# New landing margins, a later start for the transposes of x, and a fourth buffer pair in the last window, in the plan of an attention-plus-SSM kernel

## The chip, the core and the metric

One core of a Trainium2 chip runs the whole kernel. The core has five engines with an instruction queue each: TensorE (PE in the profile; PEld is its loading of weights), VectorE (DVE), ScalarE (ACT), GpSimd (POOL) and SyncE (SP). SP here only issues transfers between HBM and on-chip memory. TensorE's results land in PSUM banks, and the other engines read them there. An engine takes its instructions strictly in the order in which the program lists them; between engines there are semaphores. The metric is the time of one execution in device microseconds, lower is better, as the median of several runs. A profiled execution gives the trace from which all other numbers come.

## The reference

Two branches read the same x of 2048 x 512: softmax attention with 32 heads of 16 columns, and a state space layer (S4), that is, a convolution of every column with a kernel of 2048 steps that is built from 128 complex modes. A gate mixes the two.

```python
def _A_ref(x, wqkv, wo):
    ...
    scale = Dh ** -0.5
    scores = jnp.einsum("bhqd,bhkd->bhqk", q, k) * scale
    p = _softmax(scores, axis=-1)
    o = jnp.einsum("bhqk,bhkd->bhqd", p, v)
    return (lambda x, *d: x.transpose(*d))(o, 0, 2, 1, 3).reshape(B, S, D) @ wo

def _B_ref(u, A_re, A_im, B_re, B_im, C_re, C_im, log_dt, Dskip):
    ...
    P = jnp.exp(logdA[:, :, None] * l[None, None, :])
    K = jnp.einsum("dn,dnl,dn->dl", Cc, P, dB).real
    ...
    Yf = Uf * Kf[None, :, :, :]
    y = ...irfft2(Yf)[:, :, 0, :L]
    y = (lambda x, *d: x.transpose(*d))(y, 0, 2, 1) + u * Dskip[None, None, :]
    return y

x = A_x
g = _sigmoid((x * gate_w).sum(-1, keepdims=True))
a = _A_ref(x, A_wqkv, A_wo)
b = _B_ref(x, B_A_re, B_A_im, B_B_re, B_B_im, B_C_re, B_C_im, B_log_dt, B_Dskip)
return g * a + (1 - g) * b
```

## The kernel before

**Attention.** The scores of 32 heads, 2048 queries and 2048 keys are cut into 2048 tiles of 128 keys x 512 queries, in 32 blocks of 64 tiles; a block is four heads over 512 queries. The loop at the end of `record()` walks over 683 score groups. For each group g, `qk(g)` puts three tiles of scores into one of two PSUM buffers, SC (PE, matmul SC<-Qm,KT), and `ex(g)` lets ACT take the exponential of them into a slot of ET (line 907, ET<-SC). `pv()` then multiplies the tiles with the values, into the PSUM bank OA (PE, OA<-ET,VE). At a block's end DVE transposes OA into OT (line 978), which frees OA for the next block, and normalises: a reciprocal Rz (984), a product ON (990), and, for each pair of blocks, a second transpose into OnT (997). The masked queries Qm of a block, four rows each, are loaded by SP from gm_qd (line 735), where SP stored them before from Qs (line 1597).

**Tiles that DVE takes.** Part of the exponentials is not ACT's. A *set* is four tiles of one key tile; in each of four groups one of the three tiles belongs to the set, so that ACT's exponential there is narrow (128x1024 instead of 128x1536) and DVE turns the third tile into the bits of an exponential by one operation of 0.66 us on the scores (line 943, DZ<-SC; a *bit row* below). After the fourth bit row two *steps* (line 954, DU<-DZ and DZ<-DZ, 128x2048) refine it, each followed by matmuls into OA. A set's DZ and DU are one of the buffer pairs of its window. `WIN` lists the windows: first group, group after the last, number of buffer pairs, and how many lists of key tiles may be used. Before, there are 63 sets in three windows, 30, 5 and 28 of them. `dvq()` gives the idle time that DVE must have gathered in the plan before another set starts, by the phase the program is in (`DVQ`), and `keytile()` takes the next key tile from the current block's list while more than `LEFT` of them remain, and from the next block's otherwise.

**The state space branch** runs in the gaps of PE and on DVE. `params()` and `base()` make tables of powers. `table()` then builds 16 blocks of the powers in PT, two at a time: two copies that begin a pair (line 1222), complex products (line 1001), and one store for each block, gm_ptd<-PT (line 1239, SP). As there is one PT for a pair, the two copies of the next pair overwrite what the stores read, and wait for them. `kstage()` multiplies PT with the modes' weights (bank MB), evicts Kst (lines 1272 and 1273) and stores it in gm_kpd (line 1277). `qload()` reads the stored table back transposed (Qt, line 1251), `sstage()` makes the states SG (line 1304), `scan()` carries them along time (lines 1328 to 1342). Last come 32 *y units*: `yload()` brings Py from gm_ptd (line 1360) and four Tt from gm_kpd (line 1366), three units ahead at most; PE forms y in MB (MB<-Py,SG, then MB<-Tt,XY), DVE evicts it to Yst (line 1415), and SP stores it in gm_ytd (line 1420). XY, x in another order, is loaded by `xload()` (line 1441). `turned()` makes a transposed x: eight rounds of two transposing reads XR<-gm_xrd (line 1455) and four stores gm_xcd<-XR (line 1459), through two buffers; `ublocks()` reads it (X2, line 1469). At the end y comes back transposed (`yread()`, Yl, line 1433), the gated attention of three quarters comes back as AR (`reload()`), and `outs()` adds the two (line 1565, AR<-AR,Yl). The fourth quarter goes through the last copies behind the last exponential.

**What sets the order.** Nothing of this order is written out by hand. While the program is recorded, `Prog` keeps a planned clock for every engine and a planned end for every operation, and `Sched` holds the side work as threads of segments, each with an engine, a cost and a priority. After every exponential, `fill()` issues side work until the planned clock of ACT. It takes the segment that could start first; a segment's start is `est()`, the later of its engine's clock and `ready()`, the planned end of all that it needs. For a transfer `ready()` adds a margin to the planned landing: the one given with the transfer (`m=`), otherwise `DMARG`. So the margins delay no instruction by themselves. They decide what stands ahead of it in its engine's queue. On the chip an instruction then waits for the real landing. The two places where the margins stand:

```python
t = max(t, self.fin[(s, i)] + (.03 if s == eng else self.marg.get((s, i), DMARG) if isinstance(s, tuple) else DLAG if eng == 'PE' and s == 'DVE' else .05))
...
[(PT, i, blk)], [(ptd, blk)], c=.84, lat=4.1, m=PTM)
```

Of the kernel before, what the change touches and what calls it, by code (L numbers as in the profile page):

```python
# [24 lines left out]
ZCOL = .216 / 512  # L25
FILL = 3500
EVERY = 2
XAT = "pt0"
HWIN = 3.0
OVER = .6  # L30
DLAG = 0.6
TURN = dict(F=.105, R=.105, C=.105, H=.06)
DMARG = 1.2
PTM = 2.4
ZLAG = .6
BARE = 1
NS = 15
# [5 lines left out]
XB = 128 * (127 - math.log2(3.15037))  # L43
VKT = ((1, 5, 9, 13), (3, 7, 11))
SHAPE = ((2, 1),) * 4
LEFT = 3
VSW = 152
VSP = [len(k) * VSW for k in VKT]
VSAT = (158, 500)
WIN = ((170, 475, 2, 1), (475, 540, 3, 1), (540, 678, 3, 2))  # L50
DVQ = (("scan1", 0.2), ("scan0", 0.5), ("S15", 1.0), (None, 0.5))
BP = 2.2
DVCAP = 2.0
BUP = 1
# [33 lines left out]
class Prog:  # L88
# [65 lines left out]
    def ready(self, a):  # L154
        eng, R, W = a[1][0], a[1][2], a[1][3]
        t = 0.0
        for acc, wr in ((R, False), (W, True)):
            for b, sl, *tag in acc:
# [5 lines left out]
                for d in (st[0], st[1]) if wr else (st[0],):  # L164
                    for s, i in d.items():
                        if s != "PE" or eng != "PE":
                            t = max(t, self.fin[(s, i)] + (.03 if s == eng else self.marg.get((s, i), DMARG) if isinstance(s, tuple) else DLAG if eng == 'PE' and s == 'DVE' else .05))
        return t
# [52 lines left out]

    def dma(self, eng, fn, R=(), W=(), c=.45, lat=3.0, m=DMARG):
        if self.cap is not None:
            self.cap.append((self.dma, (eng, fn, R, W), dict(c=c, lat=lat, m=m)))
            return
        self.log.append((self.dma, self.q, (eng, fn, R, W)))
        k = self.dnext
        self.dnext = (k + 1) % NDSEM
        s = ("D", k)
        deps = self._deps(s, R, W)  # L230
        if self.dn[k]:
            deps[s] = max(deps.get(s, -1), self.dn[k])
        at = self.tm[eng]
        for s2, k2 in deps.items():
            at = max(at, self.fin[(s2, k2)] + .08)
        self.tm[eng] = at + c
        self.dn[k] += 1
        self.fin[(s, self.dn[k])] = at + c + lat
        self.marg[(s, self.dn[k])] = m
        self._record(eng, fn, deps, s, self.dn[k], R, W)  # L240
# [172 lines left out]
def declare(nc, es):  # L413
    B = {}

    def sb(name, free, dt=BF16):
        B[name] = Buf(name, "sb", free, dt)
# [9 lines left out]
    sb("ET", NS * 512)  # L427
    for w, (_, _, n, _) in enumerate(WIN):
        for r in range(n):
# [180 lines left out]
def record(nc, p, B, ins):  # L610
# [135 lines left out]
    def dvq():  # L746
        return next(n for f, n in DVQ if f is None or f in sch.flag)

    def win(x):
        return next((w for w, (lo, hi, _, _) in enumerate(WIN) if lo <= x < hi), None)  # L750

    def keys(x):
        w = win(x)
        return () if w is None else sum(VKT[:WIN[w][3]], ())

    def clear(x):
# [3 lines left out]
        mine = [i for i, st in enumerate(sets) if st["w"] == w]  # L760
        return len(mine) < WIN[w][2] or f"dvp{mine[-WIN[w][2]]}" in sch.flag

# [4 lines left out]
    def keytile(x):  # L767
        of = rem if len(rem) > LEFT else ahead
        return next(((of, q) for q in of if q % 16 in keys(x)), None)
# [27 lines left out]
    def decide(g):  # L797
        while len(tiles) < min(3 * g + 3, NSL):
            x = len(tiles) // 3
            plan["used"] = max(plan["used"], idle() - DVCAP)  # L800
            if plan["set"] is None and clear(x) and idle() - plan["used"] >= dvq():
# [3 lines left out]
                w = win(x)  # L805
                r = f"{w}{sum(st['w'] == w for st in sets) % WIN[w][2]}"
                old = [i for i, st in enumerate(sets) if st["r"] == r]
# [398 lines left out]
    def table():  # L1206
# [3 lines left out]
        for pb in range(NBLK // 2):  # L1210
# [26 lines left out]
            for i, blk in enumerate(blks):  # L1237
                yield ("SP", .5, 2)
                dma("SP", lambda e, i=i, blk=blk: e.dma_start(ptd.dram(blk * P * PTN, [[PTN, P], [1, PTN]]), PT(i * PTN, [[1, PTN]])),
                    [(PT, i, blk)], [(ptd, blk)], c=.84, lat=4.1, m=PTM)  # L1240
                sch.mark(f"pt{blk}")
# [203 lines left out]
    def turned():  # L1445
        XR, xcd = B["XR"], B["xcd"]
        for z in range(4):
            yield ("SP", .6)
            dma("SP", lambda e, z=z: e.dma_start(xcd.dram(z // 2 * P * 8192 + z % 2 * 4096 + 64 * (1 - z % 2), [[8192, P], [P, 32], [1, 64]]), wm(0, [[0, 32], [1, 64]])),
                [(wm, 0)], [(xcd, ("z", z))], c=.6, lat=6.)  # L1450
        yield ("AFTER", XAT)
        for c in range(8):
# [359 lines left out]
```

## Time and profile before

| | us |
|---|---|
| three timed runs | 850.25, 851.02, 852.69 (median 851.02) |
| the profiled execution | 850.08 |
| its span, first to last instruction | 848.3 |
| mean granted clock of TensorE | 0.982 of full speed |

The span by stages, in busy us of each engine (the view that cuts the span into windows):

| stage | span | PE | DVE | ACT | share of DMA time |
|---|---|---|---|---|---|
| start, projections, 0 to 60 | 60 | 46.5 | 45.6 | 54.3 | 0.79 |
| 60 to 200 | 140 | 109.0 | 134.6 | 140.0 | 0.36 |
| table and states, 200 to 475 | 275 | 227.2 | 260.0 | 267.9 | 0.63 |
| scans and y units, 475 to 680 | 205 | 170.8 | 193.1 | 197.8 | 0.48 |
| last y units, end, 680 to 848 | 168 | 148.9 | 149.5 | 161.2 | 0.36 |

How to read the lines below: the page gives each engine's busy time, share of the span and number of instructions. The chain of waits follows the work that ended last back from its end, at each step to what released it. A timeline row has the start and the duration in us, engine, source line, operation, output<-input, shapes, how many it stands for, and in brackets how long the engine was idle ahead of it and what ended that. A row of the groups has busy us and mean ns of one after the bar, then the idle time ahead of them with what ended most of it.

### The profile page before, as it was taken

Reading aid. Unit: us, or ns where it says so; the run is one execution under the profiler, and the core shown is the slowest. Engines: PE = TensorE matmul, PEld = TensorE weight load, DVE = VectorE, ACT = ScalarE, POOL = GpSimd, SP = SyncE. Lnnn points to the kernel's source line nnn. Section 1 sums busy time; section 2 is a strip of 40 time slices with the busy share of each in tenths; the row PEclk is TensorE's granted clock in tenths of the full one; section 3 lists DMA queues with packets and bytes.
Section 4 is the critical chain, followed back from the end, with each engine's and each line's share of the span. In section 5 each row is a group of like instructions: output and inputs, shape, how many; then the busy total and the mean of one; then the engine's idle time right before and its main releaser. Section 6 shows DMA issues by size and latency. Waiting matters only on the chain.

```text
span 848.3 us, 20990 instructions
## 1 busy us (share of the span) xinstructions
PE 702.4 (83%) x8959; PEld 255.5 (30%) x8984; DVE 782.8 (92%) x1338; ACT 821.2 (97%) x695; POOL 11.0 (1%) x13
## 2 busy tenths in 40 slices
PE   7787777777768989887788887798977779999986
PEld 3232332222112333332232332344422224434322
DVE  5799999998888999999999999999879999899995
ACT  7999999999889999999999999999979999999996
POOL 4000000000000000000000000000000000000000
PEclk9999999999899999999999999999879999999999
DMA  9750003965572568895491880166763014645203
GB/s 199 155 73 11 10 3 136 167 200 137 127 196 101 100 110 199 134 203 115 131 138 33 162 150 5 34 137 166 160 151 94 5 54 114 136 103 130 60 15 121
DMA packets 247953, 94.90 MB, mean 112 GB/s; under 512 B 222644, under 2 KB 234804, under 8 KB 245812
## 3 DMA queue, kind: packets, MB, share of 16 engines
q1 hardware_dynamic: 245988, 92.51, 49.5%
q10 hardware_dynamic: 1872, 1.05, 0.6%
q8 instruction: 70, 1.15, 0.5%
q14 instruction: 23, 0.19, 0.1%
HBM read 33.08 MB, written 35.01 MB: 80 GB/s over the span
## 4 chain that ended last, share of the span: by engine, by line
ACT 75%; DVE 11%; PE 5%; DMA 5%; SPq 2%; issue 1%; ACTq 0%; DVEq 0%
ACT ET L907 75%; DVE DZ L943 2%; PE OA L626 2%; PE SC L626 2%; DMA gm_ptd<-PT 2%; DVE tt L1001 1%; PE MB L626 1%; DMA Wk<-in_A_wqkv_dram 1%; DMA XR<-gm_xrd 1%; DVE PT L1001 1%; DMA Py<-gm_ptd 1%; DVE SG L1304 1%; SPq L1459 1%; DVE s L1331 1%; DVE ft L1001 1%
## 5 line engine op out<-in xcount | busy, mean ns | idle before, releaser
L907 ACT ACTIVATE ET<-SC 128x1536 bf16<-128x1536 f32 (+1 forms) x683 | 812.7, 1522 | 14.1 <-PE SC L626 13.6
L626 PE MATMUL SC<-Qm,KT 32*128 32x512 bf16 x2048 | 283.0, 389 | 114.8 <-ACT ET L907 99.6
L626 PE MATMUL OA<-wm 128*32 128x512 bf16 (+3 forms) x1376 | 205.8, 368 | 1.2 <-DVE wm L679 1.2
L626 PE MATMUL OA<-ET,VE 128*32 128x512 bf16 x1796 | 181.9, 397 | 6.5 <-DVE OT L978 5.9
L943 DVE TENSOR_SCALAR DZ<-SC 128x512 uint16<-128x512 f32 x252 | 167.1, 683 | 11.3 <-PE SC L626 10.6
L626 PEld LDWEIGHTS SC<-Qm,KT 32*128 32x128 bf16 x2048 | 72.4, 91 | 331.8 <-ACT ET L907 285.2
L626 PEld LDWEIGHTS OA<-ET,VE 128*32 128x32 bf16 x1796 | 46.0, 93 | 108.8 <-issue 98.3
L626 PEld LDWEIGHTS OA<-wm 128*32 128x32 bf16 (+2 forms) x1376 | 54.8, 96 | 25.5 <-issue 16.7
L954 DVE TENSOR_SCALAR DZ<-DZ 128x2048 uint16<-128x2048 uint16 x63 | 43.2, 686 | 6.5 <-PE OA L626 6.4
L1304 DVE TENSOR_SCALAR SG<-MB 128x512 bf16<-128x512 f32 x64 | 43.9, 685 | 2.7 <-PE MB L626 2.3
L626 PE MATMUL MB<-X,Qt 128*128 128x64 bf16 x512 | 42.7, 244 | 0.0
L954 DVE TENSOR_SCALAR DU<-DZ 128x2048 uint16<-128x2048 uint16 x63 | 42.6, 684 | 0.1
L1339 DVE TENSOR_TENSOR G<-s,s 128x512 f32<-128x512 f32 x60 | 41.2, 687 | 1.0
L1331 DVE TENSOR_TENSOR s<-G,MU 128x512 f32<-128x512 f32 x60 | 41.1, 684 | 0.0
L1336 DVE TENSOR_TENSOR s<-s,SG 128x512 f32<-128x512 f32 x60 | 41.0, 684 | 0.0
L1333 DVE TENSOR_TENSOR s<-G,MU 128x512 f32<-128x512 f32 x60 | 41.0, 683 | 0.0
L626 PEld LDWEIGHTS MB<-X,Qt 128*128 128x128 bf16 x512 | 28.8, 116 | 19.6 <-issue 19.6
L1001 DVE TENSOR_TENSOR ft<-FP,L 128x1024 f32<-128x1024 f32 (+1 forms) x32 | 34.2, 1086 | 0.1
L1001 DVE TENSOR_TENSOR PT<-tt,tt 128x1024 bf16<-128x1024 bf16 x48 | 32.8, 682 | 0.2
L626 PE MATMUL MB<-Py,SG 128*32 128x64 bf16 x1024 | 29.1, 234 | 3.3 <-DMA Py<-gm_ptd 3.3
L626 PEld LDWEIGHTS MB<-Py,SG 128*32 128x32 bf16 x1024 | 27.8, 168 | 11.1 <-issue 5.2
L978 DVE STREAM_TRANSPOSE OT<-OA 128x512 f32<-128x512 f32 x32 | 22.7, 709 | 4.1 <-PE OA L626 3.8
(167 smaller groups left out, 614.7 us busy)
## 6 DMA issues: line engine op xcount, KB each, us to landing
gm_ptd<-PT SPq DMA_DIRECT2D x16, 1024.0 KB, 5.7
Py<-gm_ptd SPq DMA_DIRECT2D x32, 512.0 KB, 4.5
gm_kpd<-Kst SPq DMA_DIRECT2D x16, 256.0 KB, 3.8
Tt<-gm_kpd SPq DMA_DIRECT2D x128, 32.0 KB, 3.3
gm_xrd<-in_A_x_dram SPq DMA_DIRECT2D x1, 2048.0 KB, 12.2
gm_xcd<-wm SPq DMA_DIRECT2D x4, 512.0 KB, 11.9
gm_xcd<-XR SPq DMA_DIRECT2D x32, 64.0 KB, 2.4
Wo<-in_A_wo_dram SPq DMA_DIRECT2D x4, 512.0 KB, 4.4
```

Of the source, the lines that this page charges most:

```text
L626: op("PE", lambda t: t.matmul(out(), lhsT(), rhs(), start=start, stop=stop, skip_group_check=True, **kw), R, W, c=c, lat=.15, a=a, cfg=cfg)
L907: op("ACT", lambda a: a.activation(ET(512 * e, [[1, 512 * n]]), sc(0, [[1, 512 * n]]), AF.Exp, scale=DH ** -0.5), [(sc, i, g) for i in ran ...
L943: op("DVE", lambda v: v.tensor_scalar(z.u16(512 * k, [[1, 512 * n]]), sc(512 * na, [[1, 512 * n]]), XS, XB, ALU.mult, ALU.add), [(sc, na + ...
L954: op("DVE", lambda v: v.tensor_scalar(t.u16(0, [[1, 2048]]), z.u16(0, [[1, 2048]]), float(STEP[k][0]), None, ALU.add), R, W, c=.07 + 2048 ...
L978: op("DVE", lambda v: v.transpose(OT(512 * w, [[1, 512]]), OA(0, [[1, 512]])), [(OA, 0, b)], [(OT, w, b)], c=.64)
L1001: op(eng, lambda v: v.tensor_tensor(o(), a(), b_(), f), R, W, c=c)
L1304: op("DVE", lambda v, kh=kh, part=part: v.tensor_scalar(sg(2 * SGH + SGH * part + CB * k8 + 16 * kh, [[2 * SGH, 32], [1, 16]]), MB(0, [[16 ...
L1331: op(e, lambda v: v.tensor_tensor(s2(0, W), G(0, W), MU(d0, [[0, 2], [1, 256]]), ALU.mult), key("G", "MU"), [(s2, 0)], c=F5)
L1333: op(e, lambda v: v.tensor_tensor(s3(0, W), G(256, [[-256, 2], [1, 256]]), MU(D + d0, [[D, 2], [1, 256]]), ALU.mult), key("G", "MU") + [(M ...
L1336: op(e, lambda v, so=so: v.tensor_tensor(s2(0, W), s2(0, W), sg(so, [[SGH, 2], [1, 256]]), ALU.add), [(s2, 0)] + ks, [(s2, 0)], c=F5)
L1339: op(e, lambda v: v.tensor_tensor(G(0, [[1, 512]]), s2(0, [[1, 512]]), s3(0, [[1, 512]]), ALU.add), [(s2, 0), (s3, 0)], [(G, 0)], c=F5)
L1459: dma("SP", lambda e, c=c, cc=cc: e.dma_start(xcd.dram(cc % 2 * P * 8192 + cc // 2 * (4096 + 64) + 4 * c * P, [[8192, P], [P, 4], [1, 64]] ...
```

## The change

Six numbers of the plan change; the operations and their planned costs stay.

```diff
-XAT = "pt0"
+XAT = "base0"
...
-DMARG = 1.2
-PTM = 2.4
+DMARG = 2.4
+PTM = 5.0
...
-LEFT = 3
+LEFT = 4
...
-WIN = ((170, 475, 2, 1), (475, 540, 3, 1), (540, 678, 3, 2))
-DVQ = (("scan1", 0.2), ("scan0", 0.5), ("S15", 1.0), (None, 0.5))
+WIN = ((170, 475, 2, 1), (475, 540, 3, 1), (540, 678, 4, 2))
+DVQ = (("scan1", 0.0), ("scan0", 0.5), ("S15", 1.0), (None, 0.5))
```

`DMARG` and `PTM` are the margins above: `PTM` that of the table's store, `DMARG` that of every other transfer. `XAT` is the event after which `turned()` may begin; base0 comes ahead of the first table pair. `LEFT` and `DVQ` belong to the choice of sets: a set's key tile comes from the next block while four or fewer key tiles of the current one remain, and behind the second scan DVE need not have gathered any idle time. The last window gets a fourth pair of DZ and DU. Since every choice of `fill()` depends on those before it, the order of all engines changes from the first table pair on. Now 64 sets are formed, 28, 6 and 30 in the three windows; ACT has 426 wide and 257 narrow exponentials, where it had 430 and 253.

Three places, as the order of the program lists them (line, operation, output<-inputs, shape, and x for how many in a row; numbers behind a name tell buffers of one kind apart).

DVE ahead of the refill of PT behind the table's fourth stores, before (PT's last product is the first row of line 1001 shown, FP and L make the next table, B holds what the copies read):

```order
L1001 TENSOR_TENSOR PT<-tt_167,tt_168 128x2x32x16
L929 TENSOR_SCALAR VS_54<-VE 128x608 x3
L1001 TENSOR_TENSOR ft_161<-FP,L_140 128x1024
L1272 CAST Kst<-MB 128x8x64
L1273 TENSOR_SCALAR Kst<-MB,Dp 128x8
L1001 TENSOR_TENSOR B_165<-ft_160,ft_161 128x64x8 x2
L1272 CAST Kst<-MB 128x8x64
L1273 TENSOR_SCALAR Kst<-MB,Dp 128x8
L1198 CAST B_165<-FP 128x256x8
L1222 COPY PT<-B_164 128x64x16 x2
```

The same engine and place now; the rows end with the copy, and the last product into PT stands above them:

```order
L1272 CAST Kst<-MB 128x8x64
L1273 TENSOR_SCALAR Kst<-MB,Dp 128x8
L984 RECIPROCAL Rz<-OT 128x32
L990 TENSOR_TENSOR ON<-OT,Rz 128x2x16x16
L943 TENSOR_SCALAR DZ_57<-SC 128x512
L997 STREAM_TRANSPOSE OnT_75<-ON 128x512
L943 TENSOR_SCALAR DZ_57<-SC 128x512
L943 TENSOR_SCALAR DZ_59<-SC 128x512 x4
L954 TENSOR_SCALAR DU_58<-DZ_57 128x2048
L954 TENSOR_SCALAR DU_60<-DZ_59 128x2048
L1222 COPY PT<-B_166 128x64x16
```

Eight bit rows and two steps of two sets, two Kst evictions and a normalisation now stand between the store and the copy that waits for it, in place of the products for the next table and two Kst evictions.

SP around the loads of the y unit that ran at 617 us, before:

```order
L1360 DMA Py_184<-gm_ptd 128x2x1024
L1366 DMA Tt_185<-gm_kpd 64x4x64 x2
L1420 DMA gm_ytd<-Yst_186 128x4x64
L1366 DMA Tt_185<-gm_kpd 64x4x64 x2
L1441 DMA XY2_181<-gm_xrd 64x32x64 x2
L1420 DMA gm_ytd<-Yst_186 128x4x64
L1360 DMA Py_184<-gm_ptd 128x2x1024
L1366 DMA Tt_185<-gm_kpd 64x4x64
L735 DMA Qm_52<-gm_qd 16x512 x4
L630 DMA Wo2_85<-in_A_wo_dram 128x4x512
L1420 DMA gm_ytd<-Yst_186 128x4x64
L1366 DMA Tt_185<-gm_kpd 64x4x64 x3
```

SP at the same place now:

```order
L1360 DMA Py_186<-gm_ptd 128x2x1024
L735 DMA Qm_52<-gm_qd 16x512 x4
L630 DMA Wo2_87<-in_A_wo_dram 128x4x512
L1420 DMA gm_ytd<-Yst_188 128x4x64
L1366 DMA Tt_187<-gm_kpd 64x4x64 x4
L1420 DMA gm_ytd<-Yst_188 128x4x64
L1360 DMA Py_186<-gm_ptd 128x2x1024
L1366 DMA Tt_187<-gm_kpd 64x4x64 x4
L1420 DMA gm_ytd<-Yst_188 128x4x64
L1360 DMA Py_186<-gm_ptd 128x2x1024
L1366 DMA Tt_187<-gm_kpd 64x4x64 x4
L1441 DMA XY2_183<-gm_xrd 64x32x64
```

The four Qm, Wo2 and the loads of XY2 no longer stand between a unit's Py and its last Tt: the first two stand a unit earlier, XY2 two units later.

DVE in the last stretch, before:

```order
L943 TENSOR_SCALAR DZ_67<-SC 128x512 x3
L1565 TENSOR_TENSOR AR_78<-AR_78,Yl 128x2048
L1565 TENSOR_TENSOR AR_81<-AR_81,Yl 128x2048
L1565 TENSOR_TENSOR AR_84<-AR_84,Yl 128x2048
L954 TENSOR_SCALAR DU_70<-DZ_69 128x2048
L954 TENSOR_SCALAR DU_72<-DZ_71 128x2048
L954 TENSOR_SCALAR DU_68<-DZ_67 128x2048
L954 TENSOR_SCALAR DZ_69<-DZ_69 128x2048
L954 TENSOR_SCALAR DZ_71<-DZ_71 128x2048
```

DVE in the same stretch now:

```order
L943 TENSOR_SCALAR DZ_73<-SC 128x512 x2
L943 TENSOR_SCALAR DZ_67<-SC 128x512 x3
L1565 TENSOR_TENSOR AR_83<-AR_83,Yl 128x2048
L943 TENSOR_SCALAR DZ_67<-SC 128x512
L1565 TENSOR_TENSOR AR_86<-AR_86,Yl 128x2048
L954 TENSOR_SCALAR DZ_69<-DZ_69 128x2048
L954 TENSOR_SCALAR DU_72<-DZ_71 128x2048
L954 TENSOR_SCALAR DU_74<-DZ_73 128x2048
L954 TENSOR_SCALAR DU_68<-DZ_67 128x2048
L954 TENSOR_SCALAR DZ_71<-DZ_71 128x2048
L943 TENSOR_SCALAR DZ_69<-SC 128x512 x3
L954 TENSOR_SCALAR DZ_73<-DZ_73 128x2048
```

The additions into AR, which stood together behind the last bit row, now stand one by one between bit rows; four pairs of DZ and DU (67 to 74) are in use, where there were three.

## The prediction

> **What bounds the kernel now.** I read the page first: span, busy shares, the chain that ended last.
>
> ```profile
> span 848.3 us, 20990 instructions
> PE 702.4 (83%) x8959; PEld 255.5 (30%) x8984; DVE 782.8 (92%) x1338; ACT 821.2 (97%) x695; POOL 11.0 (1%) x13
> ACT 75%; DVE 11%; PE 5%; DMA 5%; SPq 2%; issue 1%; ACTq 0%; DVEq 0%
> ```
>
> ACT, with one exponential after another, is the clock of this kernel. Its 27.1 us outside work (848.3 - 821.2) are the start, the end, and what other engines make it wait. The view of waits (who waits for whom: us in all, times, longest) shows the last:
>
> ```profile
> ACT ET L907 <- PE SC L626: 13.6, 12, 3.9
> DVE PT L1222 <- DMA gm_ptd<-PT: 5.9, 3, 2.7
> ```
>
> ACT lost 13.6 us in 12 waits for scores. The timeline puts them in four places. At two of them DVE may not refill PT until the store of the pair before has landed:
>
> ```profile
> 217.48 0.43 DVE L1222 COPY PT<-B 128x1024 bf16<-128x1024 bf16 x1 [2.72 <-DMA gm_ptd<-PT]
> 222.13 1.04 PE L626 MATMUL OA<-ET,VE 128*32 128x512 bf16 x8 [2.91 <-DVE OT L978]
> 223.77 1.45 ACT L907 ACTIVATE ET<-SC 128x1536 bf16<-128x1536 f32 x1 [2.31 <-PE SC L626]
> 225.71 1.45 ACT L907 ACTIVATE ET<-SC 128x1536 bf16<-128x1536 f32 x1 [0.49 <-PE SC L626]
> 244.70 0.43 DVE L1222 COPY PT<-B 128x1024 bf16<-128x1024 bf16 x1 [2.67 <-DMA gm_ptd<-PT]
> 253.06 1.02 ACT L907 ACTIVATE ET<-SC 128x1024 bf16<-128x1024 f32 x1 [2.15 <-PE SC L626]
> 254.57 4.37 ACT L907 ACTIVATE ET<-SC 128x1024 bf16<-128x1024 f32 x4 [0.49 <-PE SC L626]
> ```
>
> DVE stands 2.72 us, its transpose of OA (line 978) comes late by as much, PE stands before the next block's first OA matmul with the scores queued behind it, and ACT runs dry. The price of both places is 2.31 + 0.49 + 2.15 + 0.49 = 5.4 us.
>
> At the other two PE itself waits for a load of a y unit, Py or Tt:
>
> ```profile
> 592.49 0.49 PE L626 MATMUL MB<-Py,SG 128*32 128x64 bf16 x16 [2.04 <-DMA Py<-gm_ptd]
> 593.43 1.47 ACT L907 ACTIVATE ET<-SC 128x1536 bf16<-128x1536 f32 x1 [1.55 <-PE SC L626]
> 595.42 3.04 ACT L907 ACTIVATE ET<-SC 128x1536 bf16<-128x1536 f32 x2 [0.52 <-PE SC L626]
> 598.98 1.46 ACT L907 ACTIVATE ET<-SC 128x1536 bf16<-128x1536 f32 x1 [0.52 <-PE SC L626]
> 616.97 0.82 PE L626 MATMUL MB<-Py,SG 128*32 128x64 bf16 x32 [1.30 <-DMA Py<-gm_ptd]
> 620.41 0.28 PE L626 MATMUL MB<-Tt,XY 64*32 64x64 bf16 x3 [2.42 <-DMA Tt<-gm_kpd]
> 621.61 1.45 ACT L907 ACTIVATE ET<-SC 128x1536 bf16<-128x1536 f32 x1 [3.91 <-PE SC L626]
> 623.60 2.79 ACT L907 ACTIVATE ET<-SC 128x1536 bf16<-128x1536 f32 x2 [0.54 <-PE SC L626]
> ```
>
> Price: 1.55 + 0.52 + 0.52 + 3.91 + 0.54 = 7.0 us. So 12.4 of the 13.6 us hang on transfers that land after the schedule thought they would, which is what the changed numbers speak of. What is gained is read there; what is paid, wherever the new order makes another engine late.
>
> **The change part by part.** *The refill of PT.* The chain of waits holds the slowest landings:
>
> ```profile
> 237.75 6.93 DMA gm_ptd<-PT
> 321.41 8.70 DMA gm_ptd<-PT
> 586.66 5.78 DMA Py<-gm_ptd
> 617.23 3.13 DMA Tt<-gm_kpd
> ```
>
> The store at 237.75 needed 6.93 us. DVE was ready for its copy at 244.70 - 2.67 = 242.03, 4.3 us after the store went out. What DVE now does between the same store and the copies is in the order (its last rows are shown above), and the groups by form price it:
>
> ```profile
> L943 DVE TENSOR_SCALAR DZ<-SC 128x512 uint16<-128x512 f32 x252 | 167.1, 683 | 11.3 <-PE SC L626 10.6
> L954 DVE TENSOR_SCALAR DZ<-DZ 128x2048 uint16<-128x2048 uint16 x63 | 43.2, 686 | 6.5 <-PE OA L626 6.4
> L1272 DVE CAST Kst<-MB 128x512 bf16<-128x512 f32 x16 | 11.0, 684 | 0.8 <-PE MB L626 0.7
> ```
>
> Eight bit rows at 167.1/252 = 0.66 us, two steps and two Kst evictions at 0.69 make 8.1 us, the normalisation left out: more than 6.93. Counted the same way, five of the other six refills that wait for a store have 8.9 us or more, above the slowest landing, 8.70. The weak one is the third: 5.5 us of work and two waits for PE's Kst matmuls stand behind its store, so it may wait up to 6.93 - 5.5 = 1.4 us; no transpose of OA follows within twenty DVE rows, so I charge nothing for it. Saved: 5.4 us, bounds 2.7 (one place stays) and 5.4.
>
> *The y units.* SP issues in order:
>
> ```profile
> 608.31 1.84 SPq L1441 DMA_DIRECT2D XY<-gm_xrd  x2
> 612.91 2.63 SPq L735 DMA_DIRECT2D Qm<-gm_qd  x4
> ```
>
> Before, Py of the unit at 617 went out behind two XY loads (1.84 us), and its last three Tt behind four Qm (2.63), Wo and a ytd store. Now Qm and Wo stand a unit earlier, the XY loads behind the next unit, and between this Py and its last Tt nothing else stands: some 3.5 us off the wait for Tt (2.42). Py follows a ytd store that waits for the third unit before. Counted on PE, from that unit's end to this one's start lie nine score groups, five wide and four narrow, 10.7 us by the means below; an eviction and two issues (1.7) and a landing of 5.78 leave 3 us. For the unit at 592 (a wait of 2.04) I counted from the fifth unit to the eleventh: 23 groups before, 25 now, two exponentials or 2.7 us more for the same transfers. All three waits are covered, the last by 0.7 us alone; I keep a tenth of the 7.0. Saved: 6.3 us, bounds 2.6 (only the place at 592 goes) and 7.0.
>
> *Tiles given to DVE.* 64 sets instead of 63: four wide exponentials become narrow. By form:
>
> ```profile
> L907 ACT ACTIVATE ET<-SC 128x1536 bf16<-128x1536 f32 x430 | 587.6, 1728 | 11.3 <-PE SC L626 11.0
> L907 ACT ACTIVATE ET<-SC 128x1024 bf16<-128x1024 f32 x253 | 243.8, 1171 | 2.8 <-PE SC L626 2.6
> ```
>
> 587.6/430 = 1.37 and 243.8/253 = 0.96 us, so 4 x 0.40 = 1.6 us saved on ACT, certain as a count.
>
> *What it costs.* First place: the start of the first window. From the first bit row to the eighth, DVE now has two Kst evictions and four normalisation rows (lines 978, 984, 990, 997) to do as well; each taken at the Kst eviction's 0.69, an upper estimate, 7 x 0.66 + 6 x 0.69 = 8.8 us, against 7 narrow exponentials, 6.7 us. Late by 2.1 at most; I take 1.0, since DVE reaches this burst after idling and wide exponentials lie at its edge. Bounds 0 and 2.1.
>
> Second place: the end. The last window carries 30 sets instead of 28, and the three additions of line 1565 have moved:
>
> ```profile
> 821.66 2.01 DVE L943 TENSOR_SCALAR DZ<-SC 128x512 uint16<-128x512 f32 x3
> 823.59 6.68 DVE L1565 TENSOR_TENSOR AR<-AR,Yl 128x2048 bf16<-128x2048 bf16 x3
> 834.88 0.69 DVE L954 TENSOR_SCALAR DZ<-DZ 128x2048 uint16<-128x2048 uint16 x1 [2.19 <-PE OA L626]
> 840.49 0.72 DVE L978 STREAM_TRANSPOSE OT<-OA 128x512 f32<-128x512 f32 x1 [3.49 <-PE OA L626]
> ```
>
> Before, they ran after the last bit row, where DVE had time (it then idled 2.19 and 3.49 us). Now one stands between two bit rows of one set, one between two of the next, and four more bit rows follow the third. A bit row that comes 6.68/3 = 2.2 us late holds its score bank, and ACT waits with it. The first costs 2.2; the second finds ACT shifted already and adds 0.3. I take 2.5 us, bounds 0 and 4.5 (both in full). The shift and the 5.7 us of old idle cover the extra set's later steps, so the tail stays.
>
> *The moved transposes of x* (lines 1455 and 1459, now after base0) leave the crowd around the table's stores for a time when SP's queue had little to issue (rows under the last rival), and nothing reads XY until the y units begin. I charge nothing; their danger is the last rival.
>
> Sum: 848.3 - 5.4 - 6.3 - 1.6 + 1.0 + 2.5 = 838.5 us of span. The profiled run took 850.08, 1.8 over its span: **840 us**, beside a median of 851.02.
>
> **A rule weighed.** After each wait PE itself is slow:
>
> ```profile
> 595.00:601.00 6.00, 6.00 (x102) 2.70 (x98) 4.15 (x8) 4.94 (x4) 0.00 (x0) 0.59 0.55 130
> ```
>
> The granted clock is the figure before the last two. It falls to 0.59, and I put ACT's second gaps of 0.49 to 0.54 us down to that; my prices hold them. The Trainium skill (TensorE: Matmul & The Clock Gate, Part 1: The HAM clock gate) has the clock halve only after an idle window of about 3.4 us. By that rule waits of 2.9 us and less would leave the clock alone, four of the five second gaps (2.0 us) would have another cause and stay, and the sum would be 840.5 of span. The row speaks against it: 0.59 right after a wait of 2.04 us.
>
> **The rivals.** *DVE becomes the bound at the end.* Two more sets in the last window are 2 x (4 x 0.66 + 2 x 0.69) = 8.0 us of DVE work. If none of it finds idle time there, it replaces the 2.5: 838.5 - 2.5 + 8.0 = 844.0, so 846 us. For it: DVE's 92%. Against it: the idle rows above.
>
> *Half comes back.* The landings lengthen with the new queue, one PT place stays (2.7) and so does the unit at 617 (4.4, less the 0.7 already kept): 838.5 + 6.4 = 844.9, so 847 us. For it: thin margins.
>
> *The waits only move:* about 850 us. Against it: orders and distances did change.
>
> *Slower: SP's queue starves the scores.*
>
> ```profile
> 99.97 0.34 SPq L1597 DMA_DIRECT2D gm_qd<-Qs  x1
> 125.15 1.69 SPq L735 DMA_DIRECT2D Qm<-gm_qd  x4
> 196.26 2.91 SPq L1455 DMA_TRANSPOSE XR<-gm_xrd  x2
> 203.01 2.50 SPq L1455 DMA_TRANSPOSE XR<-gm_xrd  x2
> ```
>
> The moved transposes run in eight rounds that wait for their own landings, 6.7 us a round (196.26 to 203.01), and Qm loads now stand behind them; a late Qm stops PE's scores and ACT with them. At the first place four rounds and a half, 30 us, stand where SP had nothing to do between 99.97 and 125.15: Qm goes out 5 us late. From its release to its first use are some 20 exponentials, 27 us, so this decides only from rounds of some 11.5 us. Three blocks late by 6 us would make 838.5 + 18 + 1.8 = 858 us. Against it: that slack, and at later places a round at most.
>
> **How the numbers follow.** Forecast 0.64 (its own range 835 to 845: all saved and nothing paid, up to both late additions in full), DVE at the end 0.12, half back 0.10, moved 0.05, slower 0.09. What this kernel's measurement can tell from no change is 0.3%, 2.6 us: 848.5 to 853.6. Faster: 0.64 + 0.12 + 0.10 less some 0.04 of their upper ends, 0.82; same 0.08; slower 0.10. The range takes in the first three: 834 to 850.
>
> **What would show it.** Right: no wait of DVE's line 1222 for gm_ptd above 1.5 us; PE's waits for Py and Tt under 1 us together; ACT's wait for SC near 5 us, most of it beside line 1565 and at the first bit rows; granted clock near 1 from 210 to 260 and 590 to 630. Wrong: a new wait of ACT over 3 us elsewhere, above all behind Qm, or y units still waiting for their loads.

## The result, and the profile after

The changed kernel takes 841.08 us (median of 4 runs, 840.06 to 842.80) where the kernel before takes 850.72 beside it: a ratio of 0.9884, 95% interval 0.9862 to 0.9907. The forecast was 840, the range 834 to 850. The profiled execution took 841.10 us, 9.0 less than that of before.

The page of the changed kernel (span; busy time, share and instructions of each engine; the chain that ended last):

```profile
span 839.3 us, 21027 instructions
PE 696.9 (83%) x8977; PEld 253.4 (30%) x9002; DVE 788.4 (94%) x1344; ACT 818.9 (98%) x695; POOL 11.0 (1%) x13
ACT 91%; PE 5%; DVE 2%; DMA 1%; issue 0%; ACTq 0%; DVEq 0%
```

Transfers held 5% of the chain before and hold 1% now. ACT's idle time fell from 27.1 to 20.4 us (839.3 - 818.9), its busy time by 2.3: together the 9.0 us of the span. The view of waits shows which waits went:

```profile
ACT ET L907 <- PE SC L626: 6.6, 12, 1.5
ACT ET L907 <- PE OA L626: 1.5, 2, 1.2
DVE PT L1222 <- DMA gm_ptd<-PT: 1.3, 1, 1.3
```

ACT's waits for scores are 6.6 us where they were 13.6, line 1222 waits once, and no row of PE waiting for Py or Tt is left (before: 3.3 and 2.4). The timeline of the changed kernel at the places that the prediction named, and at those where ACT still waits:

```profile
213.06 33.89 ACT L907 ACTIVATE ET<-SC 128x1536 bf16<-128x1536 f32 x26
230.88 0.43 DVE L1222 COPY PT<-B 128x1024 bf16<-128x1024 bf16 x1 [1.26 <-DMA gm_ptd<-PT]
190.75 2.84 ACT L907 ACTIVATE ET<-SC 128x1536 bf16<-128x1536 f32 x2 [0.93 <-PE SC L626]
195.48 1.45 ACT L907 ACTIVATE ET<-SC 128x1536 bf16<-128x1536 f32 x1 [0.45 <-PE SC L626]
248.69 1.94 ACT L907 ACTIVATE ET<-SC 128x1024 bf16<-128x1024 f32 x2 [0.82 <-PE SC L626]
250.80 1.02 ACT L907 ACTIVATE ET<-SC 128x1024 bf16<-128x1024 f32 x1 [0.17 <-PE SC L626]
252.27 1.02 ACT L907 ACTIVATE ET<-SC 128x1024 bf16<-128x1024 f32 x1 [0.45 <-PE SC L626]
254.22 4.13 ACT L907 ACTIVATE ET<-SC 128x1536 bf16<-128x1536 f32 x3 [0.92 <-PE SC L626]
747.21 0.40 PE L626 MATMUL OA<-DZ,VS 128*32 128x512 bf16 x4 [0.40 <-DVE DZ L954]
747.86 2.37 ACT L907 ACTIVATE ET<-SC 128x1536 bf16<-128x1536 f32 x2 [1.25 <-PE OA L626]
811.87 2.06 ACT L907 ACTIVATE ET<-SC 128x1024 bf16<-128x1024 f32 x2 [1.54 <-PE SC L626]
814.17 1.02 ACT L907 ACTIVATE ET<-SC 128x1024 bf16<-128x1024 f32 x1 [0.24 <-PE SC L626]
815.70 6.61 ACT L907 ACTIVATE ET<-SC 128x1024 bf16<-128x1024 f32 x5 [0.51 <-PE SC L626]
```

The first row, 26 exponentials without a gap that the view shows (the last three of them narrow), runs over the refill at 230.88: that copy waits 1.26 us and ACT doesn't notice. The rest is in the main four places: the gate near 190 (1.4 us, and 0.15 at 197), the first window's bit rows near 250 (2.4), one spot at 748 (1.25), the additions near 812 (2.3). What DVE did ahead of the last one, the first addition and the bit row behind it:

```profile
806.88 2.28 DVE L1565 TENSOR_TENSOR AR<-AR,Yl 128x2048 bf16<-128x2048 bf16 x1
809.71 0.65 DVE L943 TENSOR_SCALAR DZ<-SC 128x512 uint16<-128x512 f32 x1
```

An addition of 2.28 us stands between two bit rows, the bit row frees its score bank late, and ACT stands still 1.54 us at 811.87.

### The profile page after: what moved, and what is told of

Same layout as the page of the kernel before. It is cut to its first block, busy times and chain, and to the rows that moved or that the text cites. A ratio compares the mean times of both kernels' runs of the same rounds, so it can differ in the third digit from the quotient of the medians.

```text
span 839.3 us, 21027 instructions
## 1 busy us (share of the span) xinstructions
PE 696.9 (83%) x8977; PEld 253.4 (30%) x9002; DVE 788.4 (94%) x1344; ACT 818.9 (98%) x695; POOL 11.0 (1%) x13
## 4 chain that ended last, share of the span: by engine, by line
ACT 91%; PE 5%; DVE 2%; DMA 1%; issue 0%; ACTq 0%; DVEq 0%
ACT ET L907 91%; PE SC L626 2%; PE OA L626 2%; DMA Wk<-in_A_wqkv_dram 1%; DVE DZ L943 1%; PE MB L626 0%; DVE DZ L954 0%; DVE AR L1565 0%; DVE OT L978 0%; ACTq L630 0%; DVE Kst L1272 0%; DVE ON L990 0%; DVE OnT L997 0%; DVE KT L716 0%; DVE fo L1776 0%
## 5 line engine op out<-in xcount | busy, mean ns | idle before, releaser
L626 PE MATMUL SC<-Qm,KT 32*128 32x512 bf16 x2048 | 279.1, 389 | 124.0 <-ACT ET L907 107.4
L943 DVE TENSOR_SCALAR DZ<-SC 128x512 uint16<-128x512 f32 x256 | 170.1, 683 | 9.5 <-PE SC L626 7.9
L1342 DVE CAST SG<-G 128x512 bf16<-128x512 f32 x60 | 25.4, 423 | 1.2
## 6 DMA issues: line engine op xcount, KB each, us to landing
gm_xcd<-wm SPq DMA_DIRECT2D x4, 512.0 KB, 10.3
```

Of the source, the lines that this page charges most:

```text
L626: op("PE", lambda t: t.matmul(out(), lhsT(), rhs(), start=start, stop=stop, skip_group_check=True, **kw), R, W, c=c, lat=.15, a=a, cfg=cfg)
L943: op("DVE", lambda v: v.tensor_scalar(z.u16(512 * k, [[1, 512 * n]]), sc(512 * na, [[1, 512 * n]]), XS, XB, ALU.mult, ALU.add), [(sc, na + ...
L1342: op(e, lambda v, so=so: v.tensor_copy(sg(so, [[SGH, 2], [1, 256]]), G(0, W)), key("G"), ks if c < NCH - 2 else [(sg, k, (h, 'G')) for k i ...
```

## The experiments

Twelve kernels, each timed in five rounds beside the kernel before on the same chip, whose medians there were 850.5 to 851.4 us. Single runs of one kernel lay up to 8 us apart, so that a difference of 2 us between two edits is not settled by these; what is read below is the interval and the place of each wait in the trace. M stands for the two margins, X for XAT, S for the other three numbers (LEFT, the buffer pair, DVQ).

| run | edits | wide exponentials | median us | ratio, 95% interval | profiled span | ACT busy | ACT idle | L1222 waits for PT's store | PE waits for Py and Tt |
|---|---|---|---|---|---|---|---|---|---|
| before | none | 430 | 850.72 | 1 | 848.3 | 821.2 | 27.1 | 5.9 | 5.7 |
| the change | M X S | 426 | 841.08 | 0.9884 (0.9862 to 0.9907) | 839.3 | 818.9 | 20.4 | 1.3 | 0 |
| e1 | M | 434 | 838.60 | 0.9862 (0.9837 to 0.9886) | 837.2 | 822.0 | 15.2 | 2.8 | 0 |
| e2 | S | 422 | 851.63 | 1.0011 (0.9994 to 1.0027) | 849.3 | 818.5 | 30.8 | 7.4 | 3.4 |
| e3 | X | 430 | 842.33 | 0.9897 (0.9871 to 0.9924) | 841.0 | 821.2 | 19.8 | 2.4 | 0.3 |
| e4 | M S | 430 | 843.53 | 0.9908 (0.9879 to 0.9938) | 842.9 | 820.8 | 22.1 | 2.8 | 0 |
| e5 | M X | 434 | 847.86 | 0.9958 (0.9940 to 0.9977) | 845.4 | 822.5 | 22.9 | 0.5 | 1.9 |
| e6 | X S | 426 | 839.05 | 0.9859 (0.9831 to 0.9887) | 834.0 | 817.6 | 16.4 | 1.4 | 0 |
| e7 | OVER .65 | 430 | 847.48 | 0.9958 (0.9941 to 0.9975) | 842.5 | 819.9 | 22.6 | 4.4 | 5.4 |
| e8 | HWIN 3.1 | 426 | 843.87 | 0.9909 (0.9884 to 0.9933) | 838.5 | 818.4 | 20.1 | 5.5 | 0 |
| e9 | M X S again | 426 | 841.73 | 0.9875 (0.9843 to 0.9908) | 840.7 | 818.9 | 21.8 | 0.7 | 0 |
| e10 | M X S, additions later | 426 | 846.07 | 0.9943 (0.9925 to 0.9962) | 841.4 | 818.3 | 23.1 | 4.1 | 0 |
| e11 | e4, other places | 430 | 840.51 | 0.9883 (0.9850 to 0.9917) | 838.7 | 820.6 | 18.1 | 2.7 | 0 |
| e12 | M, pair, DVQ | 426 | 836.99 | 0.9824 (0.9795 to 0.9854) | 833.5 | 818.3 | 15.2 | 2.7 | 0 |

Of e6, e7, e8 and e10 the profiled execution was the fastest of all runs, 3 us or so under the median. ACT idle is span less busy; the last two columns are rows of the view of waits. The last one leaves out PE's waits for XY: 1.7 us in e4, 0.4 in e1 and e11, 0.2 in e12.

**e1, the margins alone.**

```diff
-DMARG = 1.2
-PTM = 2.4
+DMARG = 2.4
+PTM = 5.0
```

> The kernel before with DMARG 2.4 and PTM 5.0 alone. It has 434 wide and 249 narrow exponentials (62 sets), so 4 x 0.40 = 1.6 us more on ACT than before. Theory of the landings (the gain is the waits behind late transfers, and the margins remove them): the two PT places (5.4 us) and the y units (7.0) go, no bit rows are crowded at the first window, one is late by about 1.4 near the end: 850.1 - 12.4 + 1.6 + 1.4 = 840.7 us, as fast as the whole change; line 1222 waits once, under 3 us, at the third refill, which has only 3.5 us of work behind its store. Theory of the tiles (the gain is DVE's extra sets and the fourth buffer pair): 850.1 + 1.6 = about 851. Theory of the transposes (the y units are relieved because the reads of x left SP's queue): PT's 5.4 go, the y units' 7.0 stay: 846.3.

Measured 838.6 us, 2 us below what the theory of the landings said, and as fast as the whole change. The view of waits of this kernel, and rows of its timeline (DVE's copies, ACT around them, PE):

```profile
DVE PT L1222 <- DMA gm_ptd<-PT: 2.8, 2, 2.1
```

```profile
227.87 0.43 DVE L1222 COPY PT<-B 128x1024 bf16<-128x1024 bf16 x1 [0.68 <-DMA gm_ptd<-PT]
230.38 0.43 DVE L1222 COPY PT<-B 128x1024 bf16<-128x1024 bf16 x1 [2.08 <-DMA gm_ptd<-PT]
222.71 20.98 ACT L907 ACTIVATE ET<-SC 128x1536 bf16<-128x1536 f32 x15
244.05 3.86 ACT L907 ACTIVATE ET<-SC 128x1536 bf16<-128x1536 f32 x3 [0.36 <-PE SC L626]
243.06 0.40 PE L626 MATMUL MB<-PT,wrb 128*32 128x512 bf16 x4 [1.18 <-DVE PT L1001]
```

DVE still waits 2.8 us at the third refill, as foreseen, and little of it reaches ACT: only work for the table stands behind that copy, so the lateness comes out 13 us later, at the Kst matmuls that wait 1.18 us for the last product into PT, with scores behind them. From 222.71 to 244.05 are 21.3 us for 15 exponentials. That is 0.8 more than 15 x 1.37, the mean of before, and 1.4 more than at the pace of the seven ahead of them (1.33 each from 213.40 on): ACT lost 0.8 to 1.4 us.

**e2, the tiles alone**: LEFT 4, four buffer pairs in the last window, DVQ 0.0.

> The kernel before with LEFT 4, the fourth buffer pair and DVQ 0.0 alone. 65 sets: 422 wide exponentials, 8 x 0.40 = 3.2 us less on ACT. Theory of the landings: the refills of PT have the same work behind their stores as before, so their 5.4 us stay; the y units now follow each other faster, so their waits of 7.0 us stay or grow, by up to 5; the last sets run late into the tail, 1 to 3 us: 847 to 855 us, no gain beyond 3. Theory of the tiles: about 841 us.

Measured 851.63: no gain. ACT's work fell by 2.7 us (821.2 to 818.5), its idle time rose by 3.7. The waits for PT have grown (7.4 us, before 5.9). Those for Py and Tt are there but smaller (3.4, before 5.7), where the theory of the landings had them stay or grow. The last sets run into the tail: ACT's first final copy waits 6.9 us, before 3.1.

```profile
DVE PT L1222 <- DMA gm_ptd<-PT: 7.4, 3, 4.2
PE MB L626 <- DMA Py<-gm_ptd: 2.5, 3, 1.3
ACT fo L1774 <- PE MB L626: 6.9, 1, 6.9
```

**e3, the transposes of x alone**: XAT from pt0 to base0.

> The kernel before with XAT base0 alone. 430 wide exponentials, as before. Theory of the landings: the refills of PT have 4.7 to 7.2 us of work behind their stores, so 3 to 6 us of ACT's waits at PT stay; the y units change their distances only by the reshuffle; late bit rows near score group 262 cost up to 2: 846 to 852 us. Theory of the transposes: the y units' 7.0 us go and PT's 5.4 stay: 843 us. The rival of the starving queue (Qm late behind the rounds of transposes): ACT waits at three blocks, 855 us or more.

Measured 842.33. The theory of the transposes met the number, but with another sum; the theory of the landings held at one refill and failed at the other. At the fourth refill DVE still waits, 2.25 us where it was 2.67, and ACT's waits behind it are still 1.8 us. At the third the wait of 2.72 is gone, because the store landed sooner. Landings of the third pair's two stores (least, median, most), of before and then of e3:

```profile
DMA to landing us min/median/max: 5.0/7.6/10.3
```

```profile
DMA to landing us min/median/max: 4.0/5.1/6.2
```

In e3 the transposes no longer run beside these stores. But e8, where they still do, has 6.7 us at most for the same pair, so what shortened the landing stays open. The late bit rows near group 262 came as that theory said: ACT waits 1.34 and 0.94 us there.

PE hardly waits for the y units (0.3 us), where that theory left them to the reshuffle. They run 350 us after the transposes, so the moved reads can't have relieved them directly, as the other theory had it; there the order alone has changed. No late Qm was seen, so the rival of the starving queue fell for this kernel.

**e4, the change without XAT.**

> The whole change but XAT stays pt0. 430 wide exponentials. Theory of the landings: both landing waits are gone (12.4 us), DVE late by 2 near group 604 and by 2 at the additions near group 667, nothing late at the first window: 850.1 - 12.4 + 4 = 841.7 us, within 2 of the whole change. Theory of the transposes: the y units' waits are back, about 847 us.

Measured 843.53. ACT hardly loses time behind the refills (0.38 us) and none for Py and Tt, as the theory of the landings expected. But PE waits 1.69 us for a load of XY at 582.12, which costs ACT 1.4, and a wait stands that no theory had:

```profile
255.18 0.75 DVE L1542 TENSOR_SCALAR AO<-MB,g 128x512 bf16<-128x512 f32 x1 [3.47 <-DMA gm_xcd<-XR]
257.18 1.02 ACT L907 ACTIVATE ET<-SC 128x1024 bf16<-128x1024 f32 x1 [2.85 <-PE SC L626]
```

AO has nothing to do with XR. The two buffers were given the same memory after the order was fixed, so the first write of AO waits for the last stores of the transposes. **e11** tests that: the order of e4, row for row, with other places.

```diff
-    best, seed = None, 1
+    best, seed = None, 4
```

> The kernel of e4 (the change with XAT pt0) with the same order on every engine, but another starting number in the search for buffer places, so that AO0 no longer lies where XR lay. In e4 DVE waited 3.47 us at line 1542 for stores gm_xcd<-XR of the transposes, and ACT lost 3.8 behind it. Theory of the shared place (the wait is from the two buffers' overlap in memory, not from the order): it goes, 843.5 - 3.8 = 839.7 us. Theory that the order itself is late there: 843.5 stays.

Measured 840.51 beside 843.53 for e4 (in ratios 0.9883 and 0.9908, whose intervals overlap). The wait of line 1542 is gone from the trace, and ACT's idle time fell from 22.1 to 18.1 us. The theory of the shared place holds for the wait. Of the 4.0 us, 3.5 are ACT's two waits behind line 1542 in e4 (2.85 and 0.66); 1.4 more went with the wait for XY, and 0.9 came back elsewhere.

**e5, margins and XAT.**

> The kernel before with DMARG 2.4, PTM 5.0 and XAT base0. Margins alone gave 838.6 us, XAT alone 842.3. 434 wide exponentials. Theory of the shared waits (both edits take away the same waits behind PT's stores and the y units' loads, so there is nothing to gain twice): 838.6 plus the late bit rows of this order, 2.4 at the first window as in the whole change and 2 near score group 388: 841 to 844 us. Theory of separate gains (each edit removes waits of its own): 850.5 - 11.9 - 8.2 = 830 us.

Measured 847.86, worse than either edit alone. So the gains are not separate; but the theory of the shared waits missed too, by 4 us. ACT's idle time is 7.7 us above e1's. Both foreseen places are there at the foreseen size: the first window (2.4) and score group 388, near 503 us (0.82 + 0.30 + 0.94 = 2.1). The first three rows show the second of them, the last two a place that was not foreseen:

```profile
502.86 1.02 ACT L907 ACTIVATE ET<-SC 128x1024 bf16<-128x1024 f32 x1 [0.82 <-PE SC L626]
504.19 1.45 ACT L907 ACTIVATE ET<-SC 128x1536 bf16<-128x1536 f32 x1 [0.30 <-PE SC L626]
506.58 4.13 ACT L907 ACTIVATE ET<-SC 128x1536 bf16<-128x1536 f32 x3 [0.94 <-PE SC L626]
621.89 0.35 PE L626 MATMUL MB<-Py,SG 128*32 128x64 bf16 x8 [1.55 <-DMA Py<-gm_ptd]
622.73 1.45 ACT L907 ACTIVATE ET<-SC 128x1536 bf16<-128x1536 f32 x1 [1.00 <-PE SC L626]
```

A y unit waits for Py again, and ACT loses 1.00 us and then 0.24, 0.43 and 0.27 more. The rest of the miss is small waits at 297, 348, 425 and 601 us (0.4 to 0.7 each). So with wider margins an order can still come out that is late elsewhere.

**e6, the change without the margins.**

> The whole change but DMARG 1.2 and PTM 2.4. 426 wide exponentials, 1.6 us less on ACT than XAT alone. Theory of the shared waits: as XAT alone, 842.3 - 1.6, plus late bit rows near group 650 (1.8) and at the additions near group 671 (2.5): 841 to 845 us, line 1222 waiting some 2 us without cost to ACT. Theory that only the margins remove the waits behind late transfers: about 849 us.

Measured 839.05: with XAT and the sets in place the margins are not needed. This is the run that takes the change's gain from the margins as their sole cause.

**e7 and e8, two reshuffles by numbers that speak of no transfer.** OVER (room for PE ahead of ACT's clock) .6 to .65; HWIN (a history of PE's work) 3.0 to 3.1.

> The kernel before with OVER .65 instead of .6, a number of the plan that speaks of no transfer; the order of everything changes a little, 430 wide exponentials as before. Theory of the distances (what counts is the work between a transfer's issue and its use, however it came about): the third and fourth refill of PT have 6.4 and 5.3 us of work behind their stores, hardly more than before, and a transpose of OA 4 to 6 us behind, so 2 to 5 of the 5.4 us stay; the y units stand about as far from their loads as before, so 2 to 7 of their 7.0 stay: 844 to 850 us. Theory of the unlucky order (any reshuffle removes the waits, and the margins were one of many): 838 to 843 us.

> The kernel before with HWIN 3.1 instead of 3.0, again no number of a transfer; 64 sets, 426 wide exponentials. Theory of the distances: PT's third to fifth refill have 6.6, 4.7 and 6.0 us of work behind their stores, with a transpose of OA 1 to 5.5 us behind, so about 5 us of ACT's waits stay there; the y units stand nearer to their loads than before, so their 7.0 stay or grow: 847 to 853 us. Theory of the unlucky order: 838 to 843 us.

e7 came out at 847.48 as the theory of the distances said: the refills of PT wait 4.4 us, one y unit 5.4. e8 came out at 843.87, which that theory had at 847 or more: the PT part was right, the y units, which I had reckoned nearer to their loads, did not wait. The theory of the unlucky order, 838 to 843, missed both, e8 by 0.9 us. So a reshuffle by itself brought 0.4 and 0.9%. In e8 the y units' waits went without any wider margin, in e7 they stayed; two neighbours are too few to say how unlucky the order of before was. e8 also shows what e1 shows from the other side:

```profile
239.79 0.43 DVE L1222 COPY PT<-B 128x1024 bf16<-128x1024 bf16 x1 [2.63 <-DMA gm_ptd<-PT]
242.74 0.43 DVE L1222 COPY PT<-B 128x1024 bf16<-128x1024 bf16 x1 [2.52 <-DMA gm_ptd<-PT]
245.02 0.68 DVE L943 TENSOR_SCALAR DZ<-SC 128x512 uint16<-128x512 f32 x1
247.49 1.02 ACT L907 ACTIVATE ET<-SC 128x1024 bf16<-128x1024 f32 x1 [3.04 <-PE SC L626]
249.51 4.13 ACT L907 ACTIVATE ET<-SC 128x1536 bf16<-128x1536 f32 x3 [1.00 <-PE SC L626]
```

Here a bit row stands behind the copy with three products between, and of 5.2 us of waiting ACT loses 4.0; in e1 it lost 0.8 to 1.4 of 2.8.

**e9, the change again**, for the chip of the last three.

> The whole change once more, on the chip of the next three, which are to be set beside it. All theories: 0.988 of the kernel before, about 841 us, ACT idle in the same places as in its first profile (the gate near 190 us, the first window near 250, the additions near 812).

Measured 841.73. The expected places of waiting are there again, the gate with 0.8 us instead of 1.5. But ACT also waits at two places that the first profile does not have, 1.02 us at 501.85 and 0.69 at 556.66. So single waits of this size come and go between executions of the same kernel.

**e10, the additions held back.**

```diff
         for blk in range(NBLK):
-            yield ("AFTER", f"yr{blk}")
+            yield ("AFTER", f"yr{blk}"); (blk == 15) and (yield ("AFTER", "g672"))
```

> The whole change, but the three additions of line 1565 may start only after score group 672, so that they no longer stand between bit rows; everything ahead of them is in the order of the change. Theory of the late bit rows (an addition of 2.28 us between two bit rows holds a score bank, and ACT and then TensorE's clock pay): ACT's idle time of 1.54 + 0.24 + 0.51 near 812 us goes, with its shadow 2.9 us: 838.2, at most 1 more for a longer tail. Theory of the moved cost (the same 6.84 us of DVE come back behind the last bit rows and lengthen the tail): 841 to 845 us.

Measured 846.07, slower than the change. The idle time near 812 us went, as the first theory said. Two of the additions now stand behind the last bit rows, and the first (at 817.14) between two sets, where it costs ACT nothing. But the work came back in the tail, as the second theory said, where ACT's first final copy waited 3.2 us and now waits 6.2. A third thing neither had: SP's rounds of transposes begin at 112.07 us (in the change at 99.66), PT's first store comes late with them, and the first refill now waits and costs ACT 1.6 us. Rows of e10, SP's issues, then DVE's, ACT's and the wait in the tail:

```profile
112.07 2.55 SPq L1455 DMA_TRANSPOSE XR<-gm_xrd  x2
156.59 0.92 SPq L1239 DMA_DIRECT2D gm_ptd<-PT  x2
160.66 0.43 DVE L1222 COPY PT<-B 128x1024 bf16<-128x1024 bf16 x1 [1.32 <-DMA gm_ptd<-PT]
163.49 0.43 DVE L1222 COPY PT<-B 128x1024 bf16<-128x1024 bf16 x1 [2.40 <-DMA gm_ptd<-PT]
166.75 1.45 ACT L907 ACTIVATE ET<-SC 128x1536 bf16<-128x1536 f32 x1 [1.59 <-PE SC L626]
```

```profile
SPq L261 <- DVE u L1001: 11.5, 1, 11.5
ACT fo L1774 <- PE MB L626: 6.2, 1, 6.2
```

The edit stands 700 us later; what it did here it did through the places: XR now shares memory with a buffer u of the parameter stage, and SP waits 11.5 us for DVE to leave it. In the change itself the same stores went out 9.7 us earlier, at 146.85. So the price of the additions between bit rows, 2.3 us, is seen to go, but nothing was won by moving them back. The tail (3.0 more) and the refill (1.6 + 0.3), less the 2.3, make up 2.6 of the 4.3 us between the medians of e10 and e9; the rest is not traced.

**e12, margins, pair and DVQ, without XAT and LEFT**, with a seed of places (4) at which AO does not lie on XR.

> The kernel before with the two margins, the fourth buffer pair and DVQ 0.0, with XAT pt0 and LEFT 3, and the places of e11. 426 wide exponentials, eight fewer than e1; the additions stand ahead of the last burst of bit rows. Theory of landings plus counts: e1's 838.6 - 8 x 0.43 - 2.1 (e1's late bit rows near group 660) + up to 2.5 at the end: 833 to 836 us, faster than both kernels. Theory of DVE as the bound at the end (two more sets, 8.0 us of DVE work, have no idle time to go to): 840 us or more.

Measured 836.99, ratio 0.9824 (0.9795 to 0.9854), a little above the 833 to 836 of the first theory: the best of all, and faster than before. Beside the change (0.9875, interval 0.9843 to 0.9908, on the same chip) it is 4.7 us ahead, though the two intervals touch.

```profile
ACT ET L907 <- PE SC L626: 0.8, 2, 0.6
ACT fo L1774 <- PE MB L626: 4.2, 1, 4.2
```

Of ACT's waits for scores 0.8 us are left of 13.6, and the two sets more than in e1 go with 1.1 more in the tail (4.2 where e1 has 3.1), not the 8.0 us of the rival.

## Why the prediction was right, and where it was not

Its number came out within 1.1 us, and the waits went at all four places. That the number fits so well is in part luck: costs of some 3 us that it had too small or not at all were balanced by 1.4 us more of gain than it counted and by small gaps. Its view of the cause was too narrow.

- **The refill of PT** (saved 5.4): the size is right, the reason in one place of two. At the fourth refill it is the work behind the store, as predicted: its copies wait for nothing, the first of them 10 us behind the store. The third refill waits 1.3 us without harm, as charged. But it was saved by its store landing in 7.8 us, where that of before took 10.3. The prediction took 8.70, from the chain of waits, for the slowest landing and did not see this one; DVE's second copy there has less time behind its store than before (6.5 us, before 7.6). That a wait at a refill costs little where no bit row or transpose of OA stands close behind it, and much where one does, is what e1 and e8 show.
- **The y units** (saved 6.3): 7.0; nothing of the waits was left, where a tenth was reserved.
- **The tiles** (1.6): ACT's busy time fell by 2.3.
- **The first window** (paid 1.0, bounds 0 and 2.1): this term was mis-sized. ACT stood 0.82 + 0.17 + 0.45 + 0.92 = 2.4 us. The lateness was near the upper bound, and PE's clock fell behind it, which the term left out though the prediction had priced just that at the other places.
- **The additions** (paid 2.5): 1.54 + 0.24 + 0.51 = 2.3.
- **The transposes** (charged nothing): no late Qm. The gate's stage, which the new order also moved, costs 1.5 us of ACT's time in front of exponentials near 190 us, and cost 0.9 at its own line 1496 before.
- **Not foreseen**: 1.25 us at 747.86. ACT waits there not for scores but for PE's OA matmuls (the releaser is OA<-ET), and ahead of these PE has a set's OA<-DZ, which waits 0.40 us for DVE's second step (the row at 747.21).

Sum: -5.4 - 7.0 - 2.3 + 2.4 + 2.3 + 1.25 + 0.6 = -8.2 of the 9.0 us; the rest is gaps too small to name.

The signs that it named came out, but for one: line 1222 waits 1.26 us at most, PE does not wait for Py or Tt, and 4.7 of the 6.6 us of ACT's waits for scores lie at the first bit rows and the additions. The granted clock is 1.00 from 590 to 630, but 0.93 from 210 to 260.

The step that does not hold is the one that tied the 12.4 us to the margins, "which is what the changed numbers speak of". The margins alone do remove them (e1). But XAT alone leaves only 1.8 of them (e3), the change without margins is as fast as with them (e6), and a number that speaks of no transfer brings 0.9 of the change's 1.2% (e8). Read from the table, the margins change the ratio by -1.4 points alone, +0.6 beside XAT, -1.0 beside the sets and +0.2 beside both. What can be said for them: with them line 1222 waited at most 2.8 us in seven profiles of eight (the eighth is e10, with its late store), without them 1.4 to 7.4 in six; and 2.8 us of it cost ACT 0.8 to 1.4 in e1. Against them: with them PE still waited 1.7 us for XY in e4 and 1.9 for Py and Tt in e5. How much of the gain is due to them and how much to leaving a bad order stays open: each setting gives one order only, and one order can't tell a rule from luck.

Of the rivals, DVE as the bound at the end showed itself only in e2 and e10, where work ran into the tail; that the waits only move, in e5. That half comes back did not happen: what is left of these waits in the change costs ACT nothing. A late queue was seen only in e10, at PT's store and not at Qm, and it cost ACT 1.9 us rather than 18.

**The rule weighed**: of the two views of the clock the row's was right here. After the late bit rows near 250 and 810 the granted clock halves within a microsecond (windows of the changed kernel, start and end, busy times, the clock behind POOL's; of each pair the first is the 3.4 us ahead of the fall):

```profile
247.60:251.00 3.40, 2.17 (x14) 0.50 (x14) 3.40 (x6) 2.42 (x4) 0.00 (x0) 1.00 0.93 352
252.00:254.00 2.00, 2.00 (x19) 0.40 (x15) 1.70 (x3) 1.02 (x1) 0.00 (x0) 0.50 0.00 0
807.40:810.80 3.40, 1.87 (x26) 0.56 (x18) 3.33 (x6) 2.94 (x4) 0.00 (x0) 1.00 0.21 70
812.00:814.00 2.00, 2.00 (x12) 0.31 (x8) 1.68 (x3) 1.92 (x2) 0.00 (x0) 0.50 0.00 0
```

PE's longest wait ahead of the second was 1.15 us, and it was busy for 2.17 and 1.87 of the 3.4 us. The Trainium skill (TensorE: Matmul & The Clock Gate, Part 1: The HAM clock gate) asks in its table for an idle window of about 3.4 us first; these rows do not agree. The length of the falls does fit such a window: they last once, twice and three times 3.4 us (251.1 to 254.5, 810.8 to 817.7, 186.2 to 196.4).

## What to carry to other kernels

A wait for a transfer costs what stands behind it in the waiting engine's queue: 1.3 us of waiting cost nothing in the change, 2.8 cost 0.8 to 1.4 in e1 and 5.2 cost 4.0 in e8, so look for the first instruction behind the wait that the bound engine needs. In this kernel, whose order a scheduler decides, each number changed was a new draw of every queue and, through the placement of buffers, of waits that the plan does not know; in such a kernel compare a change with a few neutral ones before it gets the credit. And read the gain as an account of the bound engine: its busy time by counts, its idle time place by place. Leave room in it: a second execution of the same kernel had 1.7 us at two places of its own (e9).

## What the hardware showed unexpectedly

The granted clock fell without any long wait. At 186.2 us of the changed kernel, among matmuls with one column of moving data for the gate, PE had waited 0.33 us at most in the 3.4 us before, and then ran at half speed for ten microseconds:

```profile
183.00:186.00 3.00, 2.19 (x34) 1.09 (x34) 2.90 (x5) 3.00 (x4) 0.00 (x0) 1.00 0.98 401
186.00:187.00 1.00, 0.52 (x11) 0.28 (x8) 1.00 (x2) 1.00 (x2) 0.00 (x0) 0.60 1.34 219
188.00:197.00 9.00, 9.00 (x89) 2.43 (x86) 5.18 (x13) 7.56 (x7) 0.00 (x0) 0.53 0.25 67
```

In the third row PE is busy all the time and ACT is not: for nine microseconds PE was the bound, and ACT paid 1.4 us. In e9, the same kernel again, the clock fell at the same place for 3.4 us only, and in e6 this stage shows a full clock, so what sets it off is not settled here.
